# Loads of the first three pairs on two queues, pair 2 in pieces of three rows, and a new order up to the second batch

## Chip, cores and metric

The kernel runs on one core of one Trainium2 chip. The metric is device time in microseconds (us), the median of several runs. A separate profiled execution gives the trace, in which times are counted from the start of its span.

## What is computed

Block-sparse attention (4 batches, 8 heads, 768 rows, head size 64), then a two-dimensional Fourier transform of which the real part is added to its input, then a normalised two-layer perceptron with a residual. Cut to the core:

```python
k_rep = k.reshape(B, H, 12, 64, D).mean(axis=3)              # one mean key for each block of 64
gate = einsum('bhsd,bhnd->bhsn', q, k_rep)                   # -1e9 where block n is later than the row's
sel  = argsort(gate)[..., -3:] + own block                   # blocks that a row may look at
attn = softmax(where(mask(sel) & causal, q @ k.T / 8, -1e9))
x = (attn @ v) as [B, 768, 512]
u = x + real(fft(fft(x, axis=1), axis=2))
un = (u - mean(u)) / sqrt(var(u) + 1e-6)
out = u + relu(un @ w_ch1) @ w_ch2                           # 512 -> 2048 -> 512
```

## The kernel before

The work is cut by batch (4) and, in the attention, by pairs of heads: 16 pairs P, four for each batch. Nothing is left to a scheduler: a string ORDER lists some 1,070 items, each a letter group and its indices, and the program emits them one by one. Each engine runs its own items in that order and waits only for data and buffers. Which item runs on which engine:

- Loads by SP: `Lk:P`, `Lq:P`, `Lv:P` (k, q, v of a pair), `LT` and `LF` (the tables `fs_sb` and `fd_sb` of the two Fourier steps), `Lc`, `Li`. Weights by GpSimd (POOL): `W:n` for the first layer, `X:n` for the second. The output `od` goes by SP.
- TensorE (PE): `tk:P`, `tq:P` transpose k and q (for pairs 0 to 6; from pair 7 on it is a transpose on VectorE); `g:P` is the gate product; `s:P,i` one of six tiles of scores, with the masks added by matmul (lines 485 and 497; 490 from pair 7 on); `v:P` is attention times v (L525); `y` and `m` the two Fourier steps; `xt` turns the normalised input; `w` and `c` are the two layers (L710, L735).
- VectorE (DVE): `ks:P` sums k over blocks (L359), `qc:P` copies q out of PSUM (L384 to L389), `gt`, `gx`, `gl`, `gm` make the block mask of a pair out of its gate values; `x:P` divides by the row sums; `fs`, `fd`, `f` fold the rows and columns for the Fourier step; `ty:0,1`, `tr`, `u`, `un`, `bn`, `o` follow.
- ScalarE (ACT): `kc:P` copies k out of PSUM (L370, L373), `iz` spreads the block indicators, `e:P,i` is the exp of a score tile (L507), later `nm`, `xu` and most of the `r` (ReLU).
- POOL: `kh:P` halves the block sums for the two heads, `qs:P` copies q in 16 bits, `d:P,i` masks the diagonal (L513), `vc:P` copies v in 16 bits, `fc` does the edge columns of the fold, `K:P` copies a mask from pair 7 on.

Which of four PSUM slots a tile takes, and which of three or four SBUF buffers a load of q or k takes, is listed in PLACES; a new tile waits for the readers of the old one in its slot. A buffer of v is one of two, in turn.

Loads come in two forms. Pairs in R3 bring each half of the rows as one transfer whose pieces are three rows long:

```python
def rows3(src, b, hp, h):
    return src[b, 2 * hp:2 * hp + 2].rearrange("e (h p r) d -> h p e (r d)", h=2, r=3)[h]
```

that is 768 bytes a piece, 192 KB a transfer, two transfers for a tensor of a pair. The others up to pair 6 bring each head as one transfer with pieces of one row (256 bytes, also 192 KB). A v is one transfer of 384 KB. The form decides how `tk` and `tq` transpose: 24 matmuls of 128 columns against `id32` (L338) for R3, 6 transposes (L350) otherwise.

Before the first item, `consts_first` issues k and q of pair 0 and sets constants, loads ScalarE's table, and runs nine matmuls on zeros (L772).

Of the kernel before, what the change touches and what calls it, by code (L numbers as in the profile page):

```python
# [131 lines left out]
w:0,4,2 w:0,4,0 un:0,1 w:0,5,1 Lk:7 tk:7 gx:6 gl:6,0 ks:7 gl:6,1 gm:6 d:5,3 qs:7 W:2 kh:7 d:5,1
r:0,5 w:0,6,1 r:0,6 w:0,7,2 w:0,4,1 w:0,7,0 r:0,4 w:0,7,1 r:0,7 s:6,0 e:6,0 s:6,2 e:6,2 g:7 gt:7
bn:0,1 bn:0,5 Lk:8 tk:8 gx:7 ks:8 gl:7,0 gl:7,1 gm:7 d:5,2 d:5,5 d:5,4 d:6,0 w:0,2 s:6,5 e:6,5 r:0,2
s:6,4 e:6,4 s:6,3 e:6,3 s:6,1 e:6,1 w:0,3 w:0,0 r:0,0 r:0,3 Lv:5 vc:5 kc:7 w:0,14 r:0,14 v:5 x:5
w:0,13 r:0,13 Lq:8 tq:8 Lc:0 K:7 s:7,5 e:7,5 s:7,2 e:7,2 w:0,15 r:0,15 d:6,3 d:6,4 d:6,1 d:6,5 kh:8
s:7,4 g:8 gt:8 gx:8 d:7,5 qs:8 X:0 Lv:6 vc:6 Lk:9 tk:9 gl:8,0 ks:9 Lq:9 tq:9 gl:8,1 fs:5,0 fs:5,1
gm:8 e:7,4 d:7,4 s:7,1 e:7,1 s:7,0 e:7,0 d:7,0 d:7,2 d:6,2 w:0,1 r:0,1 w:0,9 w:0,10 r:0,10 r:0,9
kc:8 bn:0,0 v:6 s:7,3 w:0,12 r:0,12 x:6 bn:0,4 bn:0,3 fs:6,0 fs:4,1 w:0,8 r:0,8 e:7,3 w:0,11 r:0,11
kh:9 X:1 qs:9 K:8 s:8,3 e:8,3 fs:4,0 g:9 gt:9 s:8,1 s:8,0 s:8,4 e:8,0 e:8,1 gx:9 gl:9,0 fs:6,1  # L140
gl:9,1 gm:9 d:7,1 Lv:7 vc:7 d:7,3 v:7 x:7 fd:6,1 fd:6,0 fs:7,1 fs:7,0 fd:7,0 bn:0,2 c:0,0,0 c:0,2,0
c:0,1,0 K:9 d:8,3 kc:9 e:8,4 Li:0 s:9,1 e:9,1 s:9,0 e:9,0 c:0,3,0 fd:7,1 fc:1 f:1,0 f:1,2 f:1,1 nv:0
nr:0 s:9,5 e:9,5 f:1,3 y:1,1,0 y:1,1,1 ty:1,1 tr:1,1 Lv:9 Lk:10 tk:10 ks:10 y:1,0,0 y:1,0,1 ty:1,0
tr:1,0 Lk:11 tk:11 ks:11 s:9,4 e:9,4 c:0,3,1 c:0,2,1 s:8,2 o:0,3 Lq:10 o:0,2 tq:10 Lk:12 m:1,2 u:1,5
e:8,2 kc:10 od:0,3 od:0,2 Lq:11 Lq:12 Lv:8 c:0,1,1 kh:10 g:10 d:8,2 d:9,5 gt:10 gx:10 u:1,4 m:1,0
u:1,0 s:9,3 e:9,3 c:0,0,1 s:8,5 e:8,5 d:9,0 kh:11 vc:9 u:1,1 tk:12 gl:10,0 m:1,1 u:1,3 u:1,2 o:0,1
gl:10,1 gm:10 tq:11 o:0,0 ks:12 nm:1,4,2 nm:1,0,2 xu:1,5 xu:1,4 un:1,4 s:9,2 e:9,2 nm:1,2,2 xu:1,1
un:1,1 c:0,4,0 c:0,4,1 o:0,4 kc:11 xu:1,3 un:1,3 xu:1,0 un:1,0 d:8,0 d:9,4 d:9,3 qs:10 d:8,1 d:9,1
d:9,2 v:9 g:11 K:10 s:10,4 e:10,4 gt:11 x:9 gx:11 gl:11,0 gl:11,1 tq:12 gm:11 c:0,5,0 xu:1,2 un:1,2
s:10,0 s:10,3 s:10,2 e:10,3 e:10,2 bn:1,5 c:0,5,1 o:0,5 bn:1,1 e:10,0 s:10,1 e:10,1 qs:11 d:8,5  # L150
d:8,4 vc:8 v:8 s:10,5 e:10,5 x:8 K:11 s:11,4 e:11,4 fs:9,0 d:10,4 s:11,2 kh:12 g:12 gt:12 e:11,2
s:11,0 s:11,1 e:11,0 e:11,1 s:11,3 e:11,3 d:11,4 d:11,1 d:10,3 d:10,1 d:11,3 d:10,0 un:1,5 w:1,11
r:1,11 fs:9,1 w:1,3 r:1,3 Lk:13 tk:13 gx:12 gl:12,0 gl:12,1 Lv:11 Lq:13 gm:12 K:12 w:1,15 s:11,5
e:11,5 d:11,0 w:1,0 w:1,14 r:1,14 kc:12 w:1,10 bn:1,2 r:1,15 ks:13 kh:13 d:11,5 d:11,2 vc:11 r:1,0
Lk:14 od:0,4 Lv:10 r:1,10 w:1,2 w:1,9 r:1,9 bn:1,4 d:10,5 qs:12 w:1,13 tq:13 r:1,2 Lv:14 bn:1,0 g:13
r:1,13 d:10,2 v:11 vc:10 bn:1,3 Lv:12 nv:1 s:12,5 w:1,12 od:0,5 e:12,5 gt:13 gx:13 Lk:15 w:1,7
r:1,12 x:11 kc:13 w:1,6 gl:13,0 r:1,7 od:0,1 fs:8,0 s:12,4 gl:13,1 Lq:14 gm:13 s:12,3 e:12,4 fs:8,1
v:10 K:13 tk:14 e:12,3 w:1,1 x:10 kc:14 qs:13 w:1,5 tk:15 Lq:15 r:1,1 w:1,4 r:1,5 fs:11,0 ks:15 nr:1
r:1,6 s:13,1 ks:14 od:0,0 s:13,5 w:1,8 e:13,5 r:1,4 fs:10,0 tq:14 s:12,2 r:1,8 fs:11,1 c:1,0,0
fd:11,1 e:13,1 tq:15 kh:15 kh:14 s:13,3 fs:10,1 s:12,1 fd:10,1 c:1,1,0 fd:11,0 e:12,1 fd:10,0 fc:2  # L160
e:13,3 f:2,1 f:2,2 s:13,0 e:12,2 f:2,3 c:1,0,1 f:2,0 e:13,0 d:12,2 d:13,3 s:12,0 d:12,3 g:15 e:12,0
d:12,5 g:14 d:13,1 c:1,1,1 gt:14 vc:14 gx:14 Lv:15 y:2,0,0 o:1,1 y:2,1,0 o:1,0 y:2,1,1 od:1,1
y:2,0,1 ty:2,1 c:1,4,0 vc:15 ty:2,0 tr:2,1 Lv:13 tr:2,0 od:1,0 m:2,1 d:12,1 d:12,0 d:13,0 m:2,0
u:2,3 u:2,2 c:1,4,1 u:2,0 nm:2,2,2 u:2,1 m:2,2 gl:14,0 nm:2,0,2 gl:14,1 xu:2,2 gm:14 bn:2,2 xu:2,3
c:1,5,0 K:14 gt:15 gx:15 c:1,2,0 o:1,4 vc:12 u:2,4 od:1,4 un:2,3 qs:14 gl:15,0 u:2,5 c:1,3,0 bn:2,3
nm:2,4,2 xu:2,5 un:2,2 bn:2,0 xu:2,1 d:13,5 s:13,4 qs:15 c:1,3,1 e:13,4 un:2,1 gl:15,1 bn:2,5 xu:2,4
un:2,5 s:13,2 gm:15 xu:2,0 c:1,2,1 e:13,2 un:2,0 kc:15 d:13,2 d:13,4 s:14,0 un:2,4 o:1,3 d:12,4
c:1,5,1 vc:13 bn:2,1 K:15 o:1,2 v:12 o:1,5 od:1,2 od:1,3 od:1,5 v:13 x:12 e:14,0 s:15,0 x:13 w:2,2
s:15,5 w:2,15 r:2,2 e:15,0 w:2,6 r:2,15 e:15,5 d:15,5 bn:2,4 s:14,1 r:2,6 w:2,8 e:14,1 s:14,5 w:2,5
d:14,1 e:14,5 r:2,8 s:14,3 r:2,5 s:15,3 w:2,14 e:15,3 d:15,3 s:15,4 r:2,14 w:2,0 e:14,3 w:2,9 r:2,0  # L170
e:15,4 s:15,1 w:2,7 r:2,9 d:15,4 d:15,0 e:15,1 s:14,2 r:2,7 w:2,4 e:14,2 nv:2 nr:2 s:15,2 w:2,10
e:15,2 r:2,4 w:2,11 w:2,3 r:2,11 d:15,2 d:15,1 s:14,4 r:2,3 v:15 e:14,4 fs:13,0 w:2,1 d:14,4 x:15
# [693 lines left out]
```

## Time and profile before

| | |
|---|---|
| median of 3 runs | 284.36 us (284.32 to 285.33) |
| the profiled execution | 284.95 us, with a span of 283.3 us |
| TensorE busy | 276.4 us, 98% of the span |
| VectorE, ScalarE, GpSimd busy | 188.7, 167.6 and 122.3 us |
| bytes moved by DMA | 33.45 MB |
| granted TensorE clock | 1.0 |

A row of the timeline or of the chain begins with the start and the length in us; then come the engine, the line of the kernel, the operation, the tile written and the tiles read, and how many instructions were merged. A bracket at the end tells how long the engine had stood idle and whose end released it. SPq, ACTq and POOLq are the queues' own instructions, the issue of a transfer among them. A group of instructions shows its busy time, the mean of one in ns, and after the bar the idle time just before them.

### The profile page before, as it was taken

To read this page: it belongs to the slowest core of one execution; us is meant where nothing else is said; L and a number is where in the kernel's file an instruction comes from. 1 tells how busy PE (TensorE), PEld (TensorE's weight loads), DVE (VectorE), ACT (ScalarE), POOL (GpSimd) and SP (SyncE) were. 2 spreads that over 40 slices of the span, in tenths; PEclk is the share of its full clock that TensorE was granted. 3 is DMA by queue.
4 is the path that set the end of the run, shared out by engine and by line. 5 is a ranking of instruction groups with operands and counts; after the bars stand their busy time and mean duration, and the time that the engine had idled before them with its cause. 6 is when DMAs were issued, how large, how long until landed. Compare 5 with 4: busy or idle time off the path is not lost.

```text
span 283.3 us, 6782 instructions
## 1 busy us (share of the span) xinstructions
PE 276.4 (98%) x2629; PEld 172.7 (61%) x2629; DVE 188.7 (67%) x568; ACT 167.6 (59%) x221; POOL 122.3 (43%) x314
## 2 busy tenths in 40 slices
PE   8999999999999999999999999999999999999995
PEld 4756677776566655556665475566575554565454
DVE  1689999998799699978979669550276452380032
ACT  2698989859869456794787634669641261343100
POOL 2164956724896726854946627711522000002000
PEclk9999999999999999999999999999999999999999
DMA  7999999999599959579497062420000042000045
GB/s 200 222 227 208 242 178 172 187 174 164 87 169 197 146 101 184 98 147 153 112 203 134 1 179 74 106 91 0 2 0 2 1 130 59 0 37 2 0 154 180
DMA packets 117040, 33.45 MB, mean 118 GB/s; under 512 B 107600, under 2 KB 113808, under 8 KB 117008
## 3 DMA queue, kind: packets, MB, share of 16 engines
q1 hardware_dynamic: 112928, 28.62, 50.1%
q0 software_dynamic: 3664, 4.19, 9.5%
q8 instruction: 20, 0.33, 0.5%
q10 hardware_dynamic: 416, 0.20, 0.2%
q14 instruction: 12, 0.10, 0.1%
HBM read 28.55 MB, written 6.29 MB: 123 GB/s over the span
## 4 chain that ended last, share of the span: by engine, by line
PE 84%; DVE 9%; POOL 3%; ACT 2%; issue 2%; DVEq 0%; POOLq 0%
PE h L710 30%; PE c L735 25%; PE sc L490 6%; PE av L525 6%; POOL qk L246 2%; PE yp L595 2%; PE sc L485 2%; DVE u L641 2%; PE tp L350 1%; PE g L408 1%; PE warmps L772 1%; PE tp L338 1%; PE mx L627 1%; PE sc L497 1%; PE c L728 1%
## 5 line engine op out<-in xcount | busy, mean ns | idle before, releaser
L507 ACT ACTIVATE pt<-sc 128x1024 f16<-128x1024 f32 (+1 forms) x96 | 83.8, 919 | 26.3 <-PE sc L490 19.4
L710 PE MATMUL h<-unT,w 128*128 128x256 f16 (+1 forms) x528 | 87.5, 321 | 0.0
L735 PE MATMUL c<-w_sb,hT 128*128 128x512 f16 x368 | 83.7, 379 | 0.0
L710 PEld LDWEIGHTS <-w 128*128 128x128 f16 x528 | 50.8, 98 | 31.0 <-issue 0.3
L735 PEld LDWEIGHTS <-hT 128*128 128x128 f16 x368 | 35.7, 98 | 40.7 <-issue 0.3
L720 ACT ACTIVATE hT<-h 128x768 f16<-128x768 f32 x48 | 37.8, 808 | 37.1 <-PE h L710 36.9
L513 POOL TENSOR_SCALAR_AFFINE_SELECT pt<-pt 128x256 f16<-128x256 f16 x96 | 38.3, 420 | 34.7 <-ACT pt L507 34.1
L747 DVE SCALAR_TENSOR_TENSOR u<-c,rs,u 128x512 f32<-128x512 f32 (+2 forms) x26 | 17.6, 701 | 35.1 <-PE c L735 32.1
L246 POOL TENSOR_SCALAR_AFFINE_SELECT qk<-mt 32x160 f16<-32x160 f16 x72 | 23.8, 351 | 19.1 <-DVE mt L462 17.6
L718 DVE TENSOR_SCALAR hT<-h 128x768 f16<-128x768 f32 x16 | 15.2, 952 | 23.7 <-PE h L710 23.5
L490 PE MATMUL sc<-qk 96*128 96x512 f16 (+3 forms) x144 | 27.2, 306 | 0.1
L525 PEld LDWEIGHTS <-pt 128*128 128x128 f16 x672 | 22.1, 97 | 2.7 <-POOL pt L513 1.0
L525 PE MATMUL av<-v,pt 128*128 128x65 f16 x672 | 23.0, 193 | 0.3 <-POOL pt L513 0.3
L246 POOL TENSOR_SCALAR_AFFINE_SELECT qk<-q 64x768 f16<-64x768 f32 (+1 forms) x25 | 21.1, 844 | 4.3 <-DVE q L386 3.3
L243 POOL TENSOR_TENSOR t<-vr,rs 128x6 f32<-128x6 f32 x12 | 2.8, 235 | 40.5 <-DVE rs L686 39.8
L490 PEld LDWEIGHTS <-qk 96*128 96x128 f16 x144 | 13.1, 98 | 8.9 <-issue 1.4
L641 DVE SCALAR_TENSOR_TENSOR u<-mx,x 128x512 f32<-128x512 f32 x24 | 15.4, 685 | 1.9 <-PE mx L628 1.8
L655 ACT ACTIVATE x<-u,nm 128x512 f16<-128x512 f32 x24 | 16.3, 715 | 0.3
L246 POOL TENSOR_SCALAR_AFFINE_SELECT v<-nat 128x768 f16<-128x768 f32 x16 | 14.6, 915 | 4.1 <-DMA nat<-in_v_dram 3.9
L675 DVE BATCH_NORM_STATS2 bst<-u 128x6 f32<-128x512 f32 x24 | 16.1, 671 | 0.0
L243 DVE TENSOR_TENSOR x<-av,rcp 128x768 f16<-128x768 f32 x16 | 15.3, 957 | 0.6
L485 PE MATMUL sc<-qk 64*128 64x512 f16 (+3 forms) x112 | 14.6, 306 | 0.8 <-DVE q L386 0.5
(105 smaller groups left out, 323.2 us busy)
## 6 DMA issues: line engine op xcount, KB each, us to landing
nat<-in_v_dram SPq DMA_DIRECT2D x16, 384.0 KB, 4.9
out_dram<-u SPq DMA_DIRECT2D x23, 256.0 KB, 2.4
nat<-in_q_dram SPq DMA_DIRECT2D x36, 96.0 KB, 3.7
nat<-in_k_dram SPq DMA_DIRECT2D x36, 96.0 KB, 3.5
nat<-in_q_dram SPq DMA_DIRECT2D x14, 192.0 KB, 4.6
nat<-in_k_dram SPq DMA_DIRECT2D x13, 192.0 KB, 4.9
w_sb<-in_moe_w_ch_dram POOLq DMA_DIRECT2D x2, 1024.0 KB, 11.9
w<-in_moe_w_ch_dram POOLq DMA_DIRECT2D x2, 768.0 KB, 7.6
```

The lines of the kernel that those rows point to most:

```text
L243: (eng or nc.vector).tensor_tensor(out=out, in0=in0, in1=in1, op=op)
L246: nc.gpsimd.affine_select(out=out, in_=in_, pattern=[[0, i] for i in n], base=0, channel_multiplier=0, compare_op=ALU.is_ge, fill=0.0)
L485: nc.tensor.matmul(ps[:, e, co:co + q1 - q0], qk[hs[e], 1, XW(P), 128 * jt:128 * jt + 128], qk[hs[e], 0, XW(P), q0:q1], start=(co == 0), s ...
L490: nc.tensor.matmul(ps[:, e, co:co + q1 - q0], qk[0:96, e, 1, 128 * jt:128 * jt + 128], qk[0:96, e, 0, q0:q1], start=True, stop=True)
L507: nc.scalar.activation(out=d["pt"][:, o:o + 2 * n].rearrange("p (e c) -> p e c", e=2), in_=d["sc", i][:, :, 0:n], func=AF.Exp, scale=0.125)
L513: nc.gpsimd.affine_select(out=dg, in_=dg, pattern=[[0, 2], [1, 128]], base=0, channel_multiplier=-1, compare_op=ALU.is_ge, fill=0.0)
L525: nc.tensor.matmul(av[:, e, 66 * st:66 * st + 65], pt[:, co:co + 128], vv[:, e, jt, 0:65], start=(cnt == 0), stop=(cnt == 20))
L641: nc.vector.scalar_tensor_tensor(out=u_t[b, kp][:, k2, :].rearrange("p (m two) -> p two m", two=2), in0=mps[:, k2, :].rearrange("p (two m) ...
L710: nc.tensor.matmul(hp[:, l:r], w1s, unT[:, dt, l:r], start=(dt == 0), stop=(dt == NDT - 1))
L720: nc.scalar.activation(out=hT, in_=hp, func=AF.Relu)
L735: nc.tensor.matmul(c_ps[b, g[0]][:, st - g[0], :], h_t[b, it][:, 128 * st:128 * (st + 1)], w2_t[0][:, it, :], start=(it == 0), stop=(it == ...
L747: nc.vector.scalar_tensor_tensor(out=o, in0=ps, scalar=st_t[b][1][:, st:st + 1], in1=o, op0=ALU.mult, op1=ALU.add)
```

## The change

- R3 becomes (0, 1, 2): q and k of pair 2 come in pieces of three rows, and tk:2 and tq:2 use the form with 24 matmuls.
- `consts_first` issues k and q of pairs 0, 1 and 2 itself, in the order k0, q0, k1, q1, k2, q2; the first half of each goes by SP, the second by ScalarE. The items Lk:1, Lk:2, Lq:1 and Lq:2 leave ORDER. Before, ScalarE issued one of these transfers and SP the other eleven.
- ORDER is new up to the middle of the second batch's first layer (the item `w:1,2`), with the same items; from there on it is unchanged. PLACES (slots and buffers) is new for the same stretch.

The diff, with ORDER cut to its first part:

```diff
-R3 = (0, 1)
+R3 = (0, 1, 2)
...
-tk:0 Lk:1 kc:0 ks:0 kh:0 tq:0 qc:0 qs:0 tk:1 kc:1 iz:0 iz:1 g:0 gt:0 gx:0 gl:0,0 gl:0,1 gm:0 Lk:2
-tk:2 Lq:1 tq:1 qc:1 kc:2 s:0,4 e:0,4 s:0,3 s:0,2 ks:1 qs:1 kh:1 Lv:0 ks:2 e:0,3 g:1 gt:1 gx:1 gl:1,0
-gl:1,1 gm:1 e:0,2 d:0,3 Lq:2 s:0,5 s:0,1 e:0,1 e:0,5 d:0,5 s:0,0 tq:2 e:0,0 kh:2 vc:0 qc:2 Lk:3 tk:3
-ks:3 d:0,2 d:0,1 qs:2 d:0,4 s:1,4 e:1,4 g:2 gt:2 gx:2 kc:3 s:1,0 e:1,0 d:1,0 kh:3 Lq:3 tq:3 qc:3
-gl:2,0 s:1,1 e:1,1 Lq:4 tq:4 qc:4 s:1,5 e:1,5 s:1,2 e:1,2 gl:2,1 gm:2 g:3 gt:3 gx:3 gl:3,0 Lk:4 tk:4
...
-s:3,5 s:4,3 e:3,5 e:4,3 s:4,2 e:4,2 d:3,1 d:3,5 v:3 x:3 fs:3,1 fs:3,0 fd:2,1 fd:3,0 fd:3,1 s:5,1
-e:5,1 W:1 Lq:6 Lk:6 LF:0 LT:0 s:5,3 e:5,3 s:4,4 e:4,4 d:4,4 s:4,0 tq:6 qc:6 s:4,1 e:4,1 s:5,2 e:5,2
-e:4,0 tk:6 kc:6 fc:0 f:0,0 f:0,1 y:0,0,0 y:0,0,1 ty:0,0 f:0,2 y:0,1,0 f:0,3 y:0,1,1 Lq:7 tq:7 ks:6
...
+tk:0 ks:0 kc:0 kh:0 tq:0 qc:0 qs:0 tk:1 ks:1 kh:1 kc:1 iz:1 iz:0 g:0 gt:0 gx:0 gl:0,0 gl:0,1 gm:0
+tk:2 tq:1 qc:1 qs:1 kc:2 s:0,4 e:0,4 ks:2 kh:2 s:0,3 e:0,3 g:1 gt:1 gx:1 gl:1,0 gl:1,1 gm:1 s:0,1
+e:0,1 s:0,2 e:0,2 d:0,2 Lq:4 tq:2 qc:2 s:1,4 s:0,5 e:1,4 Lk:3 tk:3 ks:3 e:0,5 s:1,0 e:1,0 kc:3 tq:4
+qc:4 d:0,3 g:2 gt:2 qs:2 d:0,5 s:0,0 e:0,0 Lq:3 tq:3 s:1,5 e:1,5 gx:2 qc:3 gl:2,0 gl:2,1 s:1,2 e:1,2
+s:1,3 s:1,1 e:1,1 gm:2 Lv:0 vc:0 d:0,4 d:0,1 kh:3 qs:4 d:1,0 d:0,0 d:1,2 d:1,4 g:3 gt:3 gx:3 gl:3,0
+Lk:4 tk:4 kc:4 d:1,1 Lv:1 vc:1 ks:4 qs:3 kh:4 e:1,3 d:1,3 v:0 x:0 s:2,3 e:2,3 s:2,0 e:2,0 gl:3,1 g:4
...
+Lq:5 tq:5 qc:5 qs:5 s:3,4 e:3,4 s:3,1 e:3,1 d:3,1 d:3,4 d:3,2 gm:4 fs:1,1 g:5 gt:5 gx:5 gl:5,0
+gl:5,1 fs:1,0 gm:5 s:3,0 e:3,0 d:3,0 s:3,3 e:3,3 v:2 s:3,5 e:3,5 x:2 fs:2,0 fs:2,1 fd:2,1 fd:2,0
+s:4,4 e:4,4 s:4,2 e:4,2 s:4,3 e:4,3 d:3,5 d:3,3 v:3 x:3 fs:3,0 fs:3,1 fd:3,0 fd:3,1 d:4,2 fc:0 s:5,2
+e:5,2 s:5,3 s:5,1 e:5,3 s:4,1 e:4,1 Lq:7 Lk:6 Lq:6 tq:6 qc:6 W:1 Lv:4 tk:6 s:4,5 s:4,0 kc:6 e:4,5
+d:4,5 e:4,0 e:5,1 f:0,0 LT:0 y:0,0,0 f:0,1 y:0,0,1 ty:0,0 f:0,3 f:0,2 y:0,1,0 y:0,1,1 ks:6 tq:7
...
     def consts_first():
-        for who in (1, 0):
-            src = (q, k)[who]
-            t = apool.tile([128, 2, 2, 192], FP, tag=f"nat{who}{next(at[f'nat{who}'])}", name=f"nat{who}_0", bufs=1)
-            nat[0, who] = t
-            for h, eng in ((0, nc.sync), (1, nc.scalar)):
-                (nc.sync if who == 0 else eng).dma_start(t[:, h], rows3(src, 0, 0, h))
+        for P in range(3):
+            for who in (1, 0):
+                t = apool.tile([128, 2, 2, 192], FP, tag=f"nat{who}{next(at[f'nat{who}'])}", name=f"nat{who}_{P}", bufs=1)
+                nat[P, who] = t
+                for h, eng in ((0, nc.sync), (1, nc.scalar)):
+                    eng.dma_start(t[:, h], rows3((q, k)[who], 0, P, h))
```

More of the change, by code (lines that the diff above doesn't have):

```diff
@@ L132 @@
[L132 to L172, printed above, removed]
@@ new lines @@
+d:11,0 kh:13 s:11,5 s:11,4 e:11,4 d:11,4 e:11,5 d:11,5 fs:9,0 kc:12 w:1,15 od:0,4 fs:9,1 r:1,15
+w:1,2 w:1,9 r:1,9 bn:1,4 d:10,5 qs:12 w:1,13 tq:13 r:1,2 Lv:14 bn:1,0 g:13 r:1,13 d:10,2 v:11 vc:10
+bn:1,3 Lv:12 nv:1 s:12,5 w:1,12 od:0,5 e:12,5 gt:13 gx:13 Lk:15 w:1,7 r:1,12 x:11 kc:13 w:1,6
+gl:13,0 r:1,7 od:0,1 fs:8,0 s:12,4 gl:13,1 Lq:14 gm:13 s:12,3 e:12,4 fs:8,1 v:10 K:13 tk:14 e:12,3
+w:1,1 x:10 kc:14 qs:13 w:1,5 tk:15 Lq:15 r:1,1 w:1,4 r:1,5 fs:11,0 ks:15 nr:1 r:1,6 s:13,1 ks:14
+od:0,0 s:13,5 w:1,8 e:13,5 r:1,4 fs:10,0 tq:14 s:12,2 r:1,8 fs:11,1 c:1,0,0 fd:11,1 e:13,1 tq:15
@@ new lines @@
+un:3,5 c:2,4,1 un:3,3 un:3,0 c:2,5,0 c:2,5,1 w:3,5 o:2,4 bn:3,2 w:3,15 r:3,5 o:2,2 o:2,5 w:3,3
+r:3,15 w:3,12 r:3,3 w:3,13 r:3,12 w:3,2 w:3,7 r:3,2 r:3,13 w:3,0 r:3,7 bn:3,3 w:3,11 r:3,0 bn:3,0
+w:3,10 r:3,11 bn:3,1 w:3,8 r:3,10 o:2,3 w:3,4 bn:3,4 r:3,8 od:2,3 nv:3 w:3,1 r:3,4 nr:3 w:3,6 r:3,1
+r:3,6 c:3,0,0 w:3,9 c:3,1,0 r:3,9 w:3,14 r:3,14 c:3,0,1 c:3,1,1 c:3,2,0 c:3,4,0 c:3,2,1 c:3,4,1
+o:3,2 o:3,0 od:3,2 od:2,5 o:3,1 c:3,3,0 o:3,4 od:3,1 od:2,2 od:3,4 c:3,5,0 c:3,3,1 o:3,5 od:3,5
+od:3,0 od:2,4 c:3,5,1 o:3,3 c:3,5,2 od:3,3 o:3,6 od:3,6 o:3,7 od:3,7
```

76 lines of the change are left out of this document (51 added, 25 removed).

## The prediction, made before the change was run

> **What bounds the kernel now.** I read the page first, then the busy time by stretches, then the chain of waits, then the order of instructions in the first 20 us and around 32 to 56 us.
>
> ```profile
> span 283.3 us, 6782 instructions
> ...
> PE 276.4 (98%) x2629; PEld 172.7 (61%) x2629; DVE 188.7 (67%) x568; ACT 167.6 (59%) x221; POOL 122.3 (43%) x314
> ...
> PE   8999999999999999999999999999999999999995
> ...
> DMA  7999999999599959579497062420000042000045
> ```
>
> ```profile
> 14.00:41.00 27.00, 25.70 (x468) 17.96 (x469) 24.86 (x95) 24.62 (x29) 18.86 (x39) 1.00 1.16 220
> 41.00:56.00 15.00, 13.97 (x204) 10.84 (x199) 14.57 (x31) 13.57 (x23) 9.93 (x19) 1.00 1.15 175
> 56.00:120.00 64.00, 64.00 (x610) 40.34 (x608) 55.69 (x184) 46.12 (x60) 40.36 (x99) 1.00 0.90 147
> ...
> 140.00:280.00 140.00, 140.00 (x1049) 82.87 (x1046) 70.97 (x189) 62.13 (x82) 38.16 (x107) 1.00 0.26 68
> ```
>
> The columns after the stretch are its length and the busy time of PE, PEld, DVE, ACT and POOL, then clock, DMA share and GB/s. TensorE has no gap from 56 to 120 us (64.00 of 64.00) and none from 140 to 280. Before 56 us it is not full, and DVE (24.86 of 27.00), ACT (24.62) and the DMA engines (share 1.16) are all near their end. So there are two stages: up to 56 us, where the first batch's attention and Fourier step are made, and a stage after it in which TensorE works through its list without rest. If the first stage ends earlier with the same TensorE work done, the end of the kernel moves by as much.
>
> I compared the two orders item by item at the first w (the MLP of batch 0, at 56.17 us below): the TensorE items ahead of it are the same set in both. So the question is only when this w can start. These pieces of the chain lead there:
>
> ```profile
> 5.32 2.42 PE tp L338 x24
> ...
> 9.05 1.31 PE tp L338 x24
> ...
> 20.80 0.81 PE tp L350 x6
> ...
> 38.27 0.78 POOL pt L513 x2
> ...
> 40.92 0.97 DVE x L243
> ...
> 44.73 2.59 DVE fg L243 x4
> ...
> 49.04 0.95 DVE ty L608
> ...
> 56.17 1.41 PE h L710 x12
> ```
>
> Up to 38.3 us it is a mix of ACT's exps and what feeds them; then the last mask of pair 3 (POOL), v:3 on TensorE, x:3 (40.92), and from there to 49.99 DVE almost alone.
>
> **The first loads.**
>
> ```profile
> 0.81 0.48 ACTq L761 DMA_DIRECT2D nat<-in_k_dram  x1
> ...
> 1.32 1.28 ACT L768 ACT_TABLE_LOAD   x1 [1.32 <-PEq L850]
> ...
> 4.47 2.88 SPq L303 DMA_DIRECT2D nat<-in_q_dram  x2
> ...
> 5.42 0.16 ACT L780 COPY dummy<-warmps 128x1 f32<-128x1 f32 x1 [2.60 <-PE warmps L772]
> ...
> 8.62 0.96 DVE L359 TENSOR_REDUCE kr<-tp 128x12 f32<-128x768 f32 x1 [6.13 <-ACT qk L370]
> ...
> 10.41 0.80 ACT L370 CAST qk<-tp 128x768 f16<-128x768 f32 x1 [1.44 <-PE tp L338]
> ...
> 11.05 0.48 DVE L422 STREAM_TRANSPOSE gt<-g 128x288 f32<-128x288 f32 x1 [1.01 <-PE g L408]
> ...
> 13.32 0.93 DVE L386 COPY q<-tp 128x768 f32<-128x768 f32 x1
> ...
> 13.85 5.28 ACT L507 ACTIVATE pt<-sc 128x1024 f16<-128x1024 f32 x6 [0.49 <-PE sc L497]
> ...
> 14.17 1.81 DVE L359 TENSOR_REDUCE kr<-tp 128x12 f32<-128x768 f32 x2
> ...
> 16.32 0.48 DVE L422 STREAM_TRANSPOSE gt<-g 128x288 f32<-128x288 f32 x1 [0.33 <-PE g L408]
> ```
>
> ScalarE issues six transfers instead of one: 6 x 0.48 from 0.81, then the table load of 1.28 and a small exp, ends near 5.2. Its next work waits until 5.42 for the warming matmuls anyway, so this costs nothing; if an issue took twice as long, the overrun would still have to pass 7.7, where its first copy of k can start, before it costs anything. k and q of pair 0 are not late before the change (the transposes at 5.32 follow the warming matmuls directly), so pair 0 gains nothing.
>
> For pairs 1 and 2 the loads do get earlier. SP's two issues for q of pair 1 took 2.88 us, against 0.48 for the first one on ScalarE. The Trainium skill ("DMA: Bandwidth & Descriptors", section "Issuing engines are not separate DMA queues") says that starting transfers from several engines saves only the issue time, which it calls usually small beside the transfer. Here the issue time is not small, yet no wait for q or k stands in the rows above, so the rule speaks for the third rival below.
>
> **The gate of pair 0, then of pair 1.** The row of 8.62 shows DVE's reduction of k (ks) starting when ACT's copy of the same tile ended (6.13 idle, released by qk L370): the two take turns. The new order puts ks first. For pair 0 that only swaps them. For pair 1 ks:1 also comes ahead of gt:0: it starts at 10.41 in place of kc:1 and takes 0.96, so gt:0 moves from 11.05 to about 11.3, and kc:1 from 10.41 to 11.4. Behind it on ACT stand the two copies of the block masks, kc:2, and the first exp. ACT had 0.49 idle before that exp, so it moves by 1.0 - 0.5, with the small overlaps of neighbours about 0.4: **first exp at 14.3 instead of 13.85**. In return one reduction less stands before gt:1: qc:1 and ks:2 (0.93 + 0.90) from 13.6 end at 15.4, so gt:1 is there at 15.4 instead of 16.32, **0.9 earlier on DVE**.
>
> **The transposes.** A tile in pieces of three rows takes 24 matmuls, 1.31 us at 9.05, one in the old form 6 and 0.81. tk:2 and tq:2 change form: 2 x 0.50 = 1.0 us more on TensorE. tk:2 lies in the wait for the mask of pair 0. tq:2 stands just ahead of s:1,4, which the fifth exp now needs; I count 0.3 of it as ACT's wait (bounds 0 and 0.5).
>
> **ACT up to the fourth pair's last exp.**
>
> ```profile
> L507 ACT ACTIVATE pt<-sc 128x1024 f16<-128x1024 f32 (+1 forms) x25 | 21.8, 924 | 1.8 <-PE sc L497 1.1 <-PE av L525 0.4
> L373 ACT CAST qk<-tp 128x768 f16<-128x768 f32 x3 | 2.4, 798 | 0.4 <-PE tp L350 0.4
> ```
>
> These are ACT's groups from 14.0 to 38.5 us. In 24.5 us it waited 1.8 + 0.4 = 2.2; the work took 22.3. The same exps and copies come in both orders before e:3,5. From 14.3 without any wait they end 2.2 - 0.4 = 1.8 us earlier than now; with the same waits 0.4 later. Following the new order with these durations, and with 0.4 to 0.5 us of TensorE for each score tile, I find waits of 0.3 before e:1,4, 0.2 before e:0,0 and 0.5 before kc:4 (its transposes need the tile that e:1,2 reads), and small ones: 1.2 in all. That is 2.2 - 1.2 - 0.4 = **0.6 us earlier**, in the middle of the bounds; v:3 and x:3 follow it, since DVE is 0.9 ahead.
>
> **After x:3.**
>
> ```profile
> 42.45 1.49 DVE L243 TENSOR_TENSOR zw<-sd 128x768 f16<-128x768 f16 x3
> ```
>
> fd:2,1 is one of these three and now stands before x:3, where DVE waits for v:3: 1.49 / 3 = **0.5 us less** on the way to ty. If DVE has no such wait, this is 0 (the bound above). The rest of DVE's list up to the first w is the same.
>
> **Later.** From 56 us on the orders differ up to w:1,2 of the second batch, with the same items. TensorE has no idle time there to win; what it could lose I put at 0 to 0.5.
>
> **Sum:** -0.6 - 0.5 = -1.1 us. The profiled execution took 284.95 us with a span of 283.3; less 1.1 is 283.85. The median of the runs, 284.36, lies 0.59 under that execution, so the forecast is 284.36 - 1.1 = **283.3 us**, with 282.9 to 284.1 as this case's own range.
>
> **Rivals.** *First, ACT's waits close.* DVE's lead of 0.9 reaches every gate behind it, and nothing holds the exps: -1.8 - 0.5 = -2.3, 282.1 us. For it: 1.1 of the 2.2 is waiting for scores, which wait for gates. Against it: tq:2 and the tiles of PSUM that are handed on one by one.
>
> *Second, slower: the Fourier constants come late.*
>
> ```profile
> 32.18 0.43 SPq L815 DMA_DIRECT2D fs_sb<-c_FS  x1
> 32.71 5.32 SPq L296 DMA_DIRECT2D nat<-in_q_dram  x4
> ```
>
> ```profile
> fs_sb<-c_FS SPq DMA_DIRECT2D x1, 582.0 KB, 6.3
> ```
>
> ```profile
> 45.58 0.76 PE L595 MATMUL yp<-fs_sb,fg 128*128 128x193 f16 x7
> ```
>
> ```profile
> GB/s 0 0 0 0 0 0 61 87 233 335 359 366 369 333 274 177 174 287 288 295 319 301 300 259 183 163 230 328 300 308 213 258 272 283 238 228 207 224 225 222
> ```
>
> The sine and cosine table (LT) is issued at 32.18, lands 6.3 later at 38.5, and y reads it at 45.58: 7.1 us to spare. In the new order SP issues it behind q of pair 7 (5.32 us of issuing) and v of pair 4, with the other table (LF) going behind it instead of ahead. There is a pause as well: the last row is the rate in 40 slices of the first 12 us; twelve pieces of 192 KB at 330 to 369 GB/s are in by about 9.5, and the next load, q of pair 4, must wait for its buffer until tq:0 is done at 9.05 and then flows about 1 us after its issue or later, so 1 to 2 us are lost. 38.5 + 5.3 + 1.8 (the 384 KB of v:4 at 220 GB/s) - 1.8 (LF) + 1.5 is 45.3, and y is wanted at about 45. DVE asks for y's result at 49.04 - 1.1 = 47.9, and y's own matmuls take some 2 us, so it decides from a landing at 46: each us later is one at the end. Two waits of SP for a buffer, each as long as one such load (1.8), would make it 49: 3.0 - 1.1, that is 1.9 slower, 286.2 us; at 48 it is 285.3.
>
> The weights of w, W:1, also move, behind the first batch's fold:
>
> ```profile
> 39.34 0.95 POOL L799 DMA_DIRECT2D w<-in_moe_w_ch_dram  x1
> ```
>
> ```profile
> w<-in_moe_w_ch_dram POOLq DMA_DIRECT2D x2, 768.0 KB, 7.6
> ```
>
> The fold ends at 43.94 (42.45 + 1.49), less 1.1, and POOL's four small copies stand ahead of the issue; from about 44.5 plus 7.6 they land at 52 to 53, ahead of the first w at 55. I cost this at nothing; without that margin every us is one at the end too.
>
> *Third, the change brings nothing sooner:* the loads were hidden anyway, the first exp is 0.4 late, ACT's waits stay, and only fd:2,1 counts: +0.4 - 0.5 = -0.1, 284.3 us. The Trainium skill's rule on issuing engines, named above, would give this case.
>
> **How the numbers follow.** About 0.5% (1.4 us) is what a measurement of this kernel can tell from no change. Forecast 0.38, first rival 0.32, second 0.21, third 0.09. The first is faster by over 1.4 us, the second slower, forecast and third lie within: 0.32, 0.47, 0.21. The range goes from 282.0, just under the first rival, to 285.8, inside the second; I leave out about 0.08 below and 0.11 above. Cases of both signs hold much of the chance; the forecast's own range stands above.
>
> **What would show it.** Right: first exp near 14.3 and gt:1 near 15.4; ACT's idle time from 14 to 38 near 1.2; x:3 near 40.3 instead of 40.92; two zw operations after x:3 instead of three; first h matmul near 55.1; PE full from there on. Wrong: y waiting for the table or h for the weights (a DMA as releaser on PE), v waiting on POOL for its load, or TensorE with idle time between 56 and 130 us, which would mean that the re-made order of the second batch costs something after all.

## The result, and the profile after

The changed kernel took 286.60 us (median of 9 runs, 285.72 to 287.53), the kernel before on the same chip 284.98 us (9 runs, 284.21 to 285.73). The ratio is 1.0063 with a 95% interval of 1.0046 to 1.0081: slower by 1.6 us, where 1.1 us less was forecast. The profiled execution of the changed kernel took 287.0 us.

The head of its page:

```profile
span 285.3 us, 6853 instructions
...
PE 276.5 (97%) x2665; PEld 172.9 (61%) x2665; DVE 190.9 (67%) x568; ACT 167.9 (59%) x221; POOL 121.2 (42%) x314
...
PE   8899999899999999999999999999999999999995
...
DMA  7996999958999597639995062430000042010045
```

TensorE's work is what it was (276.5 us against 276.4); the span is longer, and the second slice and the eighth are now at 8. So the loss lies early. ScalarE's timeline, from its fourth transfer to the first exp:

```profile
2.40 0.49 ACTq L761 DMA_DIRECT2D nat<-in_q_dram  x1
4.06 0.38 ACTq L761 DMA_DIRECT2D nat<-in_k_dram  x1
5.36 0.37 ACTq L761 DMA_DIRECT2D nat<-in_q_dram  x1
5.77 1.28 ACT L768 ACT_TABLE_LOAD   x1 [5.77 <-DMA nat<-in_q_dram]
...
8.08 0.35 ACTq L786 DMA_DIRECT2D indc<-c_indc  x1
8.47 0.80 ACT L370 CAST qk<-tp 128x768 f16<-128x768 f32 x1 [1.01 <-DVE q L384]
...
12.65 1.56 ACT L789 COPY indz<-indc 128x768 f16<-128x768 f16 x2 [1.70 <-DMA indc<-c_indc]
14.12 0.79 ACT L370 CAST qk<-tp 128x768 f16<-128x768 f32 x1
14.81 1.03 ACT L507 ACTIVATE pt<-sc 128x1024 f16<-128x1024 f32 x1
```

The first four transfers start 0.5 us apart. The fifth and the sixth do not: ScalarE stood from 2.9 to 4.06 and from 4.44 to 5.36 before it could issue them, and the table load, which the forecast had over by 5.2, began at 5.77. The load of the block indicators, `indc`, comes behind all this on the same queue, landed at 12.6, and ScalarE waited 1.70 us for it.

The second place is around tr, the turn of the Fourier step. The view of its line, then GpSimd's timeline beside it:

```profile
L615 DVE COPY tr<-ty x2: 556/1068/1581, 50.5 to 52.0; 128x768 f16<-128x768 f16 x2
...
  PE mx L627: 0.7, 1
```

```profile
50.09 0.80 POOL L799 DMA_DIRECT2D w<-in_moe_w_ch_dram  x1
50.90 0.91 POOL L246 TENSOR_SCALAR_AFFINE_SELECT v<-nat 128x768 f16<-128x768 f32 x1
```

In the kernel before the same two copies take 405 and 555 ns. Here the first takes 1,581: it ends at 52.03, 0.22 us after GpSimd's cast of v (vc:4) ended at 51.81, and TensorE waits for it. In the order before, vc:4 ran from 51.73 on, after tr.

**A trap in comparing the two profiles.** How fast the first transposes of k run differs between executions of one kernel. In the kernel before, then in the run b_vc4_meets below, whose order up to 48 us is the same:

```profile
L338 PE MATMUL tp<-id,nat x28: 272/421/476, 5.2 to 9.0; 128*64 128x128 f32 x28
```

```profile
L338 PE MATMUL tp<-id,nat x48: 272/273/323, 5.0 to 8.9; 128*64 128x128 f32 x48
...
12.65 1.02 ACT L507 ACTIVATE pt<-sc 128x1024 f16<-128x1024 f32 x1 [0.49 <-PE sc L497]
```

The three durations are the shortest, the middle and the longest, in ns. I read them as TensorE's clock, although the granted clock of both profiles is 1.00 in these microseconds: it reached full speed late in the profiled execution of before (middle 421, longest 476), early in that of b_vc4_meets (273 and 323), and the first exp comes at 13.85 in the one and at 12.65 in the other. From there to the end the two traces run 1.1 to 1.2 us apart. The Trainium skill ("TensorE: Matmul & The Clock Gate", Part 1) says that the clock is released by a free-running window, so that the moment depends on where the window stands when the first matmul comes. These traces agree that the moment differs between executions; that such a window decides it, no run here shows. The changed kernel's trace had the early release (longest 323). At equal clock its first exp is therefore 2.2 us late (14.81 against 12.65), not 1.0. One step takes the clock out altogether: from the start of pair 1's k transposes (tk:1) to the first exp it is 4.97 us in before (8.88 to 13.85), in b_vc4_meets (7.68 to 12.65), and 4.98 in b_fd, at either clock. In the changed kernel it is 7.21 (7.60 to 14.81).

I therefore compare stretches that start at an event. From the rows of each profile: the longest of those matmuls in ns (about 475 late, 323 early), then in us the first exp, from there to the first u, and from the first matmul of w to the first c of batch 1; last the ratio of the times.

| kernel | clock | first exp | to first u | first w to c of batch 1 | ratio [95%] |
|---|---|---|---|---|---|
| before | 476 | 13.85 | 37.26 | 96.7 | 1 |
| after | 323 | 14.81 | 37.62 | 97.3 | 1.0063 [1.0046, 1.0081] |
| a_vc4_later | 476 | 14.19 | 36.82 | 97.4 | 1.0019 [1.0003, 1.0035] |
| a_vc4_act2 | 323 | 13.10 | 36.87 | 97.4 | 0.9996 [0.9976, 1.0016] |
| a_indc_first | 323 | 15.56 | 38.42 | 97.6 | 1.0106 [1.0084, 1.0129] |
| a_vc4_indc_sp | 476 | 14.60 | 36.72 | 97.4 | 1.0023 [1.0003, 1.0044] |
| a_old_loads | 476 | 13.89 | 37.92 | 97.0 | 1.0067 [1.0041, 1.0093] |
| a_vc4_old_loads | 323 | 13.51 | 37.35 | 96.9 | 1.0009 [0.9987, 1.0030] |
| b_loads | 476 | 14.60 | 37.85 | 96.8 | 1.0050 [1.0030, 1.0069] |
| b_act2 | 323 | 13.09 | 37.83 | 96.7 | 1.0011 [0.9991, 1.0032] |
| b_r3 | 323 | 13.27 | 38.17 | 96.8 | 1.0008 [0.9984, 1.0033] |
| b_fd | 476 | 13.67 | 37.15 | 96.7 | 0.9994 [0.9970, 1.0019] |
| b_vc4_meets | 323 | 12.65 | 37.25 | 96.7 | 0.9988 [0.9969, 1.0007] |
| hyb279 | 476 | 13.87 | 36.90 | 96.7 | 1.0010 [0.9997, 1.0024] |
| hyb372 | 323 | 13.08 | 36.86 | 98.8 | 1.0072 [1.0055, 1.0089] |
| hyb272 | 473 | 13.54 | 37.09 | 96.7 | 0.9987 [0.9970, 1.0005] |

The clock column tells only that a matmul was slow, not for how long: the first k tile took 2.49 us in before, 2.37 in a_vc4_later, 2.05 in hyb279, 1.7 to 1.8 in b_loads, hyb272 and a_vc4_indc_sp, and 1.53 in all traces with the early clock.

Names with a_ start from the changed kernel, those with b_ from the kernel before.

### The profile page after: what moved, and what is told of

The parts are those of the page before. It is cut to its first block, busy times and chain, and to the rows that moved or that the text cites. A ratio compares the mean times of both kernels' runs of the same rounds, so it can differ in the third digit from the quotient of the medians.

```text
span 285.3 us, 6853 instructions
## 1 busy us (share of the span) xinstructions
PE 276.5 (97%) x2665; PEld 172.9 (61%) x2665; DVE 190.9 (67%) x568; ACT 167.9 (59%) x221; POOL 121.2 (42%) x314
## 4 chain that ended last, share of the span: by engine, by line
PE 79%; DVE 10%; DMA 5%; ACT 2%; issue 1%; POOL 1%; ACTq 0%; DVEq 0%
PE h L710 28%; PE c L735 27%; PE sc L490 7%; PE av L525 4%; DMA nat<-in_k_dram 2%; PE yp L595 2%; DMA indc<-c_indc 2%; DMA unT<-x 1%; PE mx L627 1%; PE sc L485 1%; PE mx L628 1%; DVE x L243 1%; DVE u L641 1%; PE c L728 1%; PE tp L350 1%; DVE sd L243 1%
## 5 line engine op out<-in xcount | busy, mean ns | idle before, releaser
L710 PE MATMUL h<-unT,w 128*128 128x256 f16 (+1 forms) x528 | 88.4, 321 | 0.3 <-DMA unT<-x 0.3
```

Of the source, the lines that this page charges most:

```text
L710: nc.tensor.matmul(hp[:, l:r], w1s, unT[:, dt, l:r], start=(dt == 0), stop=(dt == NDT - 1))
```

## The experiments

**ScalarE's transfers and indc.** First, `indc` ahead of everything on ScalarE:

```diff
     def consts_first():
+        nc.scalar.dma_start(indc, dr["indc"].ap())
...
-        nc.scalar.dma_start(indc, dr["indc"].ap())
```

> The changed kernel with one line moved: ScalarE issues the load of the block indicators (indc) ahead of its six pieces of k and q instead of behind them. Theory 1 (the load of indc stands behind six transfers and the table load on ScalarE's queue, so the block masks are ready only at 14.2 and the first exp starts at 14.81): indc lands before 6, the masks are made at about 11, the first exp starts at 13.5 to 13.8, x:3 and the first w come 0.8 to 1.1 us earlier, and the kernel is 0.8 to 1.1 us faster than the changed one (285.5 to 285.8 where that is 286.6). Theory 2 (the new order itself is slow: reduction of pair 1 ahead of its gate, 24 matmuls of tq:2 ahead of s:1,4): the first exp moves, but gates and score tiles come no sooner, and the time changes by less than 0.3 us.

It got slower still, 1.0106. `indc` no longer made anyone wait, but the sixth transfer of k and q, now the seventh on this queue, was issued only at 7.93, the table load began at 8.34, and the first exp came at 15.56. So `indc`'s place is not the whole of it: what stands behind the held transfers moves with them.

**vc:4 away from tr.** W:0 and vc:4 go three items down in the new order:

```diff
-... d:5,3 d:4,0 d:5,1 W:0 vc:4 d:4,3 d:5,2 d:4,1 v:4 ...
+... d:5,3 d:4,0 d:5,1 d:4,3 d:5,2 d:4,1 W:0 vc:4 v:4 ...
```

> The changed kernel with the items W:0 and vc:4 moved behind d:4,1, so that GpSimd's copy of v (0.91 us) no longer runs while DVE makes the two reversed copies tr. Theory 3 (a 16-bit operation of DVE that meets such a copy on GpSimd is held until it ends: one tr took 1.58 us instead of 0.5): both tr take 0.5 us, the first u comes about 1.0 us earlier, first w 0.9 to 1.1 earlier, and the kernel is as much faster than the changed one. Theories 1 and 2: tr has another cause, no change over 0.2 us.

tr is back at its old length, and the ratio falls from 1.0063 to 1.0019, some 1.2 us. W:0 and vc:4 moved together, so this run does not tell them apart:

```profile
L615 DVE COPY tr<-ty x2: 325/442/559, 50.0 to 50.2; 128x768 f16<-128x768 f16 x2
```

**Loads alone, order alone.** b_loads is the old order with the new loads, a_old_loads the new order with the old loads.

```diff
 # b_loads: the kernel before with
-R3 = (0, 1)
+R3 = (0, 1, 2)
 # and the new loop of consts_first; Lk:1, Lk:2, Lq:1, Lq:2 leave ORDER
 # a_old_loads: the changed kernel with R3 = (0, 1), the old loop,
 # and Lk:1 Lq:1 Lk:2 Lq:2 at the head of ORDER
```

> The kernel before with its old order, and only the loads of the change: k and q of three pairs as twelve transfers by SP and ScalarE, pair 2 in pieces of three rows (Lk:1, Lk:2, Lq:1, Lq:2 left out of the order). Theory 1: indc is late here too (first exp at 14.8 to 15.0 instead of 13.85), and the kernel is 0.8 to 1.3 us slower than before. Theory 2 (the loss is in the order): within 0.5 us of before.

> The changed kernel with its new order, and the loads of the kernel before: pair 0 as before, then k and q of pairs 1 and 2 by SP alone in the order k1, q1, k2, q2, pair 2 in pieces of one row (6 transposes instead of 24 matmuls). Theory 1: indc is not late, first exp at 13.6 to 14.0, and the kernel is 0.8 to 1.3 us faster than the changed one, close to before. Theory 2: as slow as the changed one, within 0.4 us. If pair 2 now lands too late for tk:2 and tq:2, PE shows a wait for a load before 18 us.

Each alone costs about what the whole change costs (1.0050 and 1.0067). They cost it in different places: b_loads has its first exp at 14.60, a_old_loads has a slow tr (556 and 1,595 ns). With old loads and vc:4 moved, nothing can be told from before:

> The new order with W:0 and vc:4 behind d:4,1 and the loads of the kernel before (pair 2 in pieces of one row, pairs 1 and 2 by SP). Theories 1 and 3 together (what the change lost is the meeting of vc:4 and tr, 1.2 us, and the loads): span within 0.5 us of before (282.5 to 283.3). If the order has another loss (theory 2): span 283.8 or more.

Ratio 1.0009. So within the order's part it is W:0 and vc:4 (1.0067 to 1.0009). The wait for a load that was named beforehand came too: with k of pair 2 behind q of pair 1 on SP's queue, TensorE waited for it ahead of tk:2, 0.22 us in a_old_loads and 1.21 in a_vc4_old_loads, whose first exp comes 6.17 us after tk:1.

**ScalarE issues two transfers instead of six**, SP the other ten, in the new order with vc:4 moved and in the old order:

```diff
-                    eng.dma_start(t[:, h], rows3((q, k)[who], 0, P, h))
+                    (eng if P == 0 else nc.sync).dma_start(t[:, h], rows3((q, k)[who], 0, P, h))
```

> The changed kernel with W:0 and vc:4 behind d:4,1 (as in the run before), and ScalarE issuing only the two second halves of pair 0; the other eight of its twelve-list transfers' partners, those of pairs 1 and 2, all go by SP. Theory 1 in its new form (ScalarE's issues of its fifth and sixth transfer block its queue until 5.7, and table load, first copies and the load of indc stand behind them): the table load is over by 3.7, indc is issued near 5.5, the first exp starts at 13.5 to 13.9 instead of 14.2 to 14.8, and the span falls by 0.3 to 0.8 us against the kernel with vc:4 moved alone. Theory 2 (transposes in 24 matmuls and the order hold the gates): first exp earlier, but less than 0.2 us of it reaches x:3.

> The kernel before with its old order, the twelve first loads up front in pieces of three rows, but ScalarE issuing only the two of pair 0 and SP the other ten. Theory 1: the first exp is back at 13.7 to 14.0, and of the 1.4 us that the loads cost with six transfers on ScalarE at least 0.7 are gone. Theory 2 (what costs in the old order is the form with 24 matmuls: tq:2 ahead of s:1,4 gave ACT a wait of 1.07): the time stays 0.8 to 1.4 us over before.

The first exp comes at 13.1 in both, and 5.43 and 5.44 us after tk:1. The ratios fall from 1.0019 to 0.9996 and from 1.0050 to 1.0011: by these the held transfers cost 0.7 us in the new order and 1.1 in the old one, though the intervals of each two overlap, the second barely. With vc:4 moved too, the loss is gone from the time; what the new order was forecast to gain is not there. At equal early clock the span of a_vc4_act2 is still longer than that of b_vc4_meets, 282.8 us against 282.1; the first w comes at the same time in both (54.97 and 54.98), so the 0.7 lie behind it.

What held the issues stands in the view of SP's waits in after, up to 7 us:

```profile
SPq L761 <- DMA nat<-in_k_dram: 0.9, 1, 0.9
...
SPq L761 <- DMA nat<-in_q_dram: 0.7, 1, 0.7
```

They waited for earlier transfers to land. In after the fifth on each queue started when the first on that queue had landed, and the sixth when the second had: on SP at 3.75 and 4.84, after landings at 3.7 and 4.8, on ScalarE at 4.06 and 5.36, after 4.0 and 5.3. The four other traces with six transfers on each queue show the same within 0.1 us. So the sixth on ScalarE waits until its half of q of pair 0 is there, and that moves from execution to execution. It is no limit of four for a queue: in a_vc4_act2 SP issued six without a pause, and its seventh, the ninth in all, was the first to be held, until 4.51. What sets the number was not traced. SP has nothing behind its held transfers that is wanted at once.

**Three-row pieces alone**, R3 = (0, 1, 2) in the kernel before and nothing else:

> The kernel before with only R3 = (0, 1, 2): pair 2 in pieces of three rows, loads otherwise issued as before. Theory 1: the first exp stays near 13.9; TensorE has 1.0 us more to do, of which at most 0.3 shows: 0 to 0.3 us slower. Theory 2: the 24 matmuls of tk:2 and tq:2 stand ahead of score tiles that ACT waits for, 0.5 to 1.0 us slower.

The time is not to be told from before (1.0008); first exp to first u is 0.9 us longer, 38.17. The first exp is late as well, 5.43 us after tk:1 and not 4.97, since it waits for its scores behind the 24 matmuls:

```profile
13.27 5.33 ACT L507 ACTIVATE pt<-sc 128x1024 f16<-128x1024 f32 x6 [0.94 <-PE sc L497]
```

At the same early clock b_r3 has its first u at 51.44 and a span of 283.6 us, b_vc4_meets 49.90 and 282.1. So in the trace the form costs 1.5 us. The medians hide it in part: nine of the 12 runs of b_r3 lie in the lower of its two groups of spans (283.3 to 283.7, and 284.2 to 284.7), while the spans of before spread from 281.8 to 285.5 about a median of 283.1, and what lies outside the span is less in b_r3 (last section).

**Is it indc or ScalarE's own work?** The changed kernel with vc:4 moved and `indc` issued by SP:

```diff
-        nc.scalar.dma_start(indc, dr["indc"].ap())
+        nc.sync.dma_start(indc, dr["indc"].ap())
```

> The changed kernel with vc:4 behind d:4,1 (time ratio to before 1.0019) and the load of indc issued by SP right behind its six pieces instead of by ScalarE; ScalarE's six pieces stay. Theory 1a (what delays the first exp is indc, whose issue stood behind ScalarE's held ones, so that ScalarE waited 1.70 us for its landing at 12.65 us): indc lands before 10.9 us, ScalarE does not wait for it, the first exp comes at 13.1 us or earlier (14.81 in after) although the table load still begins only at 5.8 to 6.6 us; time 0.6 to 1.0 us under the run with vc:4 alone, ratio 0.998 to 1.000, as where ScalarE issued two pieces only (0.9996). Theory 1b (the held issues delay ScalarE's own work, the table load and the copies behind it): first exp at 14.0 to 14.3 and ratio 1.001 to 1.003, as with vc:4 alone. Rival: SP's queue is held in the same way, indc is issued at 7 us or later and lands after 12 us: no change either.

ScalarE's timeline, and TensorE's second k tile:

```profile
6.85 0.38 ACTq L761 DMA_DIRECT2D nat<-in_q_dram  x1
7.25 1.28 ACT L768 ACT_TABLE_LOAD   x1 [7.25 <-DMA nat<-in_q_dram]
...
8.78 0.16 ACT L780 COPY dummy<-warmps 128x1 f32<-128x1 f32 x1
...
12.44 1.56 ACT L789 COPY indz<-indc 128x768 f16<-128x768 f16 x2
```

```profile
9.00 1.53 PE L338 MATMUL tp<-id,nat 128*64 128x128 f32 x24 [0.66 <-ACT dummy L780]
```

Theory 1b holds in the ratio, 1.0023, and the first exp is 0.3 us later than it gave. Nobody waits for `indc` here, yet the first exp is at 14.60. The sixth transfer was held until 6.85, and behind it stood ScalarE's own list: the table load, and the copy that frees the PSUM slot of the warming matmuls. tk:1 waited for that slot. The sixth transfer was issued at 5.36, 6.15, 6.85 and 7.93 in the four traces with six transfers on ScalarE in the new order (after, a_vc4_later, a_vc4_indc_sp, a_indc_first). What it costs differs from execution to execution. In the last two, tk:1 waited for the warming slot, 0.66 and 1.25 us. In the first it was `indc` that came last, and in b_loads too (1.59 us). In a_vc4_later the late clock hid it all: the copy that frees the slot was done at 8.25, before tk:1 could start at 8.76, and the first exp follows tk:1 by 5.43 us, as with two transfers. ScalarE's first copy of k, in a_vc4_later and in hyb279, which issues two, shows the same, 0.32 us apart as their first k tiles are:

```profile
8.66 0.80 ACT L370 CAST qk<-tp 128x768 f16<-128x768 f32 x1 [0.41 <-DVE kr L359]
```

```profile
8.34 0.80 ACT L370 CAST qk<-tp 128x768 f16<-128x768 f32 x1 [2.77 <-DVE kr L359]
```

The rival's part is true too: SP's sixth was held until 6.60 and it issued `indc` at 8.89.

**The cast of v beside tr, in the kernel before.** vc:4 goes four places up on GpSimd, with its load Lv:4 ahead of it; nothing else moves:

```diff
-... d:4,1 d:4,2 d:4,0 d:5,0 Lv:4 d:4,5 vc:4 v:4 ...
+... d:4,1 Lv:4 vc:4 d:4,2 d:4,0 d:5,0 d:4,5 v:4 ...
```

> The kernel before, with nothing but vc:4, GpSimd's cast of v from f32 to f16, moved four places up on its engine, behind the d:4,1 that starts at 49.32 us, so that it runs from about 49.75 to 50.65 us, beside the two tr copies (0.88 us together, from 49.89). Theory of the meeting (a 16-bit VectorE copy that meets such a cast is held until it is over): the two tr take 1.6 to 2.0 us together, the longer one over 1 us; the first h matmul moves from 56.1 to about 56.9 to 57.1, and the time is 0.7 to 1.0 us longer, ratio 1.0025 to 1.0035. Rival (in after the copies were long for another reason, such as their place behind ty and what the cores' other queues did): tr 0.44 us each as before, ratio 1.000.

```profile
L615 DVE COPY tr<-ty x2: 327/690/1052, 48.7 to 48.9; 128x768 f16<-128x768 f16 x2
```

```profile
48.72 1.05 POOL L246 TENSOR_SCALAR_AFFINE_SELECT v<-nat 128x768 f16<-128x768 f32 x1 [0.20 <-DMA nat<-in_v_dram]
```

The mechanism is there, without W:0 next to it: the second copy took 1.05 us and ended 0.2 after the cast. The first, which began 0.05 us before the cast (48.67 and 48.72), took its usual 0.33. The price was not there. The two copies took 1.30 together and not 1.6 to 2.0, and behind them nothing moved (first exp to first u 37.25 against 37.26), since u waited for TensorE anyway in the kernel before:

```profile
51.11 0.69 DVE L641 SCALAR_TENSOR_TENSOR u<-mx,x 128x512 f32<-128x512 f32 x1 [0.34 <-PE mx L628]
```

The time was not longer, 0.9988. The theory's 0.7 to 1.0 us fail here: by these rows the meeting costs only what lies past that cover.

**Is the gain lost behind the first w?** hyb279 and hyb372 keep after's order (with both repairs) up to xu:0,3 and up to bn:0,0 and go on in before's; hyb272 changes over after un:0,2 and renames the PSUM slots so that no tile waits longer for its slot.

> The order of after up to the copies of the first batch's normalised rows, just ahead of the first h matmul, with W:0 and vc:4 behind d:4,1 and ScalarE issuing only the first pair's two pieces (all as in the run with both repairs, whose first h matmul stood at 55.0 us); from there on the items that remain, in before's order. Theory A (the re-made order behind the first h matmul costs 0.6 to 0.7 us between 55 and 152 us, which is why the forecast's 1.1 us at the first h matmul did not reach the end): first h matmul at 55.0, first c matmul of the first batch at 88.1 (before: 89.2), first c of the second batch near 151.7 (before 152.8), span 282.2, time ratio to before 0.996 to 0.997. Theory B (a lead at the first h matmul is taken up by what comes later whatever the order, ScalarE or VectorE by then being the bound): first c at 88.8 to 89.2, ratio 0.999 to 1.000, as with both repairs.

> As the hybrid before, but after's order is kept for longer, through the first scores of the eighth pair (some 10 to 20 us past the first h matmul), and before's order follows from there. Theory A: first h matmul at 55.0; what after's order loses by this point (0.4 us were lost between the first h matmul and the first c matmul) is lost, the rest is not: first c at 88.1 to 88.5, ratio 0.996 to 0.998. Theory B: as with both repairs, first c 88.5 to 89.2 and ratio 0.999 to 1.000.

> The first hybrid again with its seam mended: after's order (vc:4 behind d:4,1, ScalarE issuing two pieces) up to un:0,2, then what remains in before's order, the four PSUM places renamed so that no tile of the second part has a shorter wait for its place than in either kernel. In the first hybrid the first h matmul waited 0.78 us for a place that before's numbering gave it. Theory A (the re-made order behind the first h matmul costs 0.6 to 0.7 us): from first h to first c matmul 33.1 us as in before (33.5 in after's order), from there to the second batch's first c 63.6 (63.8 to 63.9), time 0.5 to 0.7 us under the kernel with both repairs (284.73), ratio 0.997 to 0.998. Theory B (a lead is taken up later whatever the order): ratio 0.9995 to 1.001.

The two first hybrids were spoilt by their seams. In hyb279 the first w stood waiting:

```profile
PE h L710 <- DVE unT L668: 0.8, 1, 0.8
```

In hyb372 TensorE waited 0.8 us for a transposed q and 0.5 for a ReLU between its first w and first c. hyb272 has no seam. Its stretch from the first w to batch 1's first c is 96.7 us as in before, against 97.4 with after's order and loads; that part of theory A holds in the trace. It is not the order alone, though: after's order with the old loads has 97.0 and 96.9 (a_old_loads, a_vc4_old_loads). One named piece is a wait in batch 1's first layer, 0.3 to 0.5 us, that the five kernels with after's whole order and new loads have and no other:

```profile
PE h L710 <- DMA unT<-x: 0.3, 1, 0.3
```

In time, hyb272 gave 284.55 us and 0.9987 [0.9970, 1.0005], 0.2 us under a_vc4_act2, not the 0.5 to 0.7 expected, and the intervals overlap. It is the fastest of the kernels that keep the new order, but not shown to be faster than before; none of these is.

**fd:2,1 alone**, the forecast's surest half microsecond, in the kernel before:

```diff
-... fs:2,1 fs:2,0 fd:2,0 s:3,5 ... x:3 fs:3,1 fs:3,0 fd:2,1 fd:3,0 ...
+... fs:2,1 fs:2,0 fd:2,0 fd:2,1 s:3,5 ... x:3 fs:3,1 fs:3,0 fd:3,0 ...
```

> The kernel before with nothing but fd:2,1 moved on VectorE from behind x:3 and fs:3 to behind fd:2,0, ahead of x:3: the step that the forecast put at -0.5 us. By the forecast: from first exp to first u 36.75 us (before 37.26), ratio 0.998. Rival, from before's VectorE rows: zw ends at 40.51 and x:3 starts at 40.65 as soon as v:3's matmul (39.17 to 40.61) is over, so only 0.14 us stand free there; x:3 comes 0.4 to 0.5 us later by as much as the work behind it grows shorter, first exp to first u 37.1 to 37.3, ratio 0.9995 to 1.000.

The rival's numbers came: first exp to first u 37.15 us, against 37.26, and 0.9994. VectorE's rows:

```profile
40.10 1.03 DVE L243 TENSOR_TENSOR zw<-sd 128x768 f16<-128x768 f16 x2
41.05 0.23 DVE L536 RECIPROCAL rcp<-av 128x12 f32<-128x12 f32 x1
```

x:3's reciprocal now follows the second zw directly, 0.58 us later after the first exp than in before (27.38 against 26.80). The step moved work from behind x:3 to ahead of it, and only 0.1 us of it was free time.

## Why the prediction was wrong

**The first step failed: "this costs nothing".** It priced six transfers at the 0.48 us of the first. The first four kept to that; the fifth and sixth were held, which no row of before could show for ScalarE, though its rows had a sign: SP's two issues for q of pair 1 took 2.88 us, 2.36 of it the first. I read that as a cost of SP's that the change would remove. (There the issue itself is long and no wait is named, so whether it is the same hold is open.) What the changed kernel shows is no price of an issue at all: the fifth and sixth wait until the first and second have landed. I also counted only the table load behind the six; the copy that frees the warming slot and the issue of `indc` stand there too. The margin named was 5.42, at the worst 7.7. In the five traces with six transfers the table load and its small exp were over between 7.1 and 9.8: past 5.42 in all, past 7.7 in three. Price: nothing (a_vc4_later) to 1.8 us (after) of the first exp, by execution, and by the medians 0.7 us of the time in the new order and 1.1 in the old.

**The forecast of 14.3 for the first exp** was +0.4. With ScalarE's transfers out of the way it is 13.10 against 12.65 at the same early clock, +0.45: the right size, and by the mechanism described. In a_vc4_act2 ScalarE's second copy of k waits for ks:1, and from there to the exp it never stands idle:

```profile
10.19 0.80 ACT L370 CAST qk<-tp 128x768 f16<-128x768 f32 x1 [1.44 <-DVE kr L359]
```

The same chain stands in a_old_loads, without the 24 matmuls of tk:2 (5.37 us from tk:1 to the exp). The form of tk:2, which the forecast put into a wait, would have made the exp as late without ks:1's new place: 5.43 in b_r3, where the order is the old one. The two run side by side, so the second costs nothing beside the first; in the old order the wait that the forecast put tk:2 into is not there. The 13.09 of b_act2 is a third case, ScalarE's wait of 0.95 us for `indc`. gt:1 did come sooner: 1.0 us after the first exp (15.82) where it had been 2.5 (16.32).

**The transposes** were put at 0.3 us. b_act2 and b_r3 show first exp to first u longer by 0.6 and 0.9 us in the old order. Against the 0.3 forecast that is two to three times as much; in the new order it was not measured alone.

**ACT's waits fell, but x:3 did not come sooner.** The group of the exps from 14.0 to 38.5 us, where 1.8 stood before:

```profile
L507 ACT ACTIVATE pt<-sc 128x1024 f16<-128x1024 f32 (+1 forms) x24 | 20.8, 919 | 0.9 <-PE sc L497 0.5
```

With 0.4 before kc that is 1.3; the forecast said 1.2. (The stretch begins 0.8 us before the first exp of after.) Yet from the first exp to x:3's reciprocal it took 26.98 us against 26.80. What released v:3 is in TensorE's rows, first after, then before:

```profile
39.99 1.44 PE L525 MATMUL av<-v,pt 128*128 128x65 f16 x42 [0.32 <-DVE x L243]
```

```profile
39.17 1.44 PE L525 MATMUL av<-v,pt 128*128 128x65 f16 x42 [0.33 <-POOL pt L513]
```

VectorE had taken over: v:3 waited for x:2. The sentence "v:3 and x:3 follow it, since DVE is 0.9 ahead" was the error. At x:2 nothing was left of that lead: it starts 24.17 us after the first exp (38.98), against 24.21 before (38.06), v:3 0.14 sooner, and then fd:2,1 stood ahead of x:3. Where between gt:1 and x:2 the lead went was not traced.

**fd:2,1** moved as described (two zw behind x:3, not three), and brought 0.1 alone instead of 0.5. The forecast's own bound, "if DVE has no such wait, this is 0", was the case.

**"The rest of DVE's list up to the first w is the same"** was true of VectorE's list and missed GpSimd's: W:0 and vc:4 came next to tr. Price: 0.8 us in the stretch to the first u (37.62 against 36.82) and 1.2 in the time. The 0.4 us between the two were not traced. With that mended, the new order does gain 0.4 us in the stretch over before, and 1.0 over the old order with the same loads; the later first exp takes the 0.4 back.

**Later** was bounded by 0.5; it is 0.6 to 0.7 with the new loads (97.3 and 97.4 against 96.7) and 0.2 to 0.3 with the old ones. Why the first loads matter that late was not traced.

**The agreement at the first w is an accident.** 55.1 was forecast, and a_vc4_act2 has 55.0. But b_vc4_meets, with before's order, also has 55.0: it is the early clock, not the 1.1 us.

**The rivals.** ACT's waits closed about as the forecast had it, not as the first rival did. The second was not it: the sine and cosine table was issued at 37.27, some 5 us later than before, and neither y nor h waited for a load up to the first c. The third, that the loads were hidden anyway, is right on its point for the order of loads in before (b_act2 and b_r3 did not gain), but the time went above it. On the Trainium skill's rule ("DMA: Bandwidth & Descriptors", section "Issuing engines are not separate DMA queues"), that issuing from more engines saves only issue time: these runs agree, and add that an engine which also computes pays for it when its issues are held.

## What to carry to other kernels

The cost of a transfer on an engine's queue is not its first issue times the count: read what stands behind the last one in that engine's own list, and expect issues to be held once several large transfers are on their way (here, with eight of 192 KB out, until one of the first had landed). When an order is re-made, look at what each step's neighbours on the other engines are, not only at its own list. And before a step ahead of a waiting instruction is called free, measure how long the engine really stands idle there.
